# Carrying fourteen output columns over to the next steps, three heads per unit in the last steps, and kept tokens in five blocks of a two-layer recurrent attention kernel

## The chip, the core and the metric

The kernel runs on one core of one Trainium2 chip. A core has TensorE (PE, matrix products, with its weight loads listed apart as PEld), VectorE (DVE), ScalarE (ACT), GpSimd (POOL) and SyncE (SP); the last two also issue most of the transfers here. The metric is the device time of one execution in microseconds, as the median over several executions.

## The reference

There are two layers of the same kind, with the same weights. Each layer is a recurrent attention over segments of 32 tokens with 8 memory rows, followed by a gated feed-forward block (FFN). 2048 tokens of width 512 make 64 segments; there are 32 heads of width 128; the FFN is 1792 wide.

```python
for s in range(n_seg):                      # 64 segments, one after another
    h = concat([mem, x[32*s:32*s+32]])      # 8 + 32 = 40 rows
    q, k, v = h @ Wq, h @ Wk, h @ Wv        # 32 heads
    p = softmax(mask(q k^T * scale))        # memory rows seen by all, the rest causal
    o = (p v) @ Wo
    mem = o[:8]                             # the next segment's memory
    outs.append(o[8:])
# block B: (sigmoid(g) * u) @ w_down with g = h @ w_gate, u = h @ w_up
x = x + A(layernorm(x)); x = x + B(layernorm(x))     # layer 1
x = x + A(layernorm(x)); x = x + B(layernorm(x))     # layer 2
```

Only the 8 memory rows bind segment s+1 to segment s. Everything else of a segment depends on its own tokens.

## The kernel before, in words

**Steps.** `trace` emits 70 steps (`emit_step(t)`, t = 0 to 69). Step t computes segment t of the first layer (job j = 0) and segment t - 6 of the second (j = 1), as far as they exist: steps 0 to 5 have layer 1 alone, steps 6 to 63 both layers side by side in one moving operand of 80 columns, steps 64 to 69 layer 2 alone with 40 columns. Columns 0 to 39 belong to layer 1, 40 to 79 to layer 2; the last `NE` = 14 columns are the last 14 tokens of layer 2's segment. The last two two-layer steps are t = 62 and 63.

**Inside a step.** 32 heads go in groups of up to six. Line names are those of the profile of the kernel before:

- L874: Q and K of three heads, 8 weight-loaded matmuls a head; L910: scores. ACT casts Q and K to `qku`.
- L924 to L945: mask, maximum, subtraction, exponential, sum, reciprocal and product, on DVE with the exponential on ACT.
- L956: the probabilities of a *unit* (two or three heads side by side) are transposed on PE; L1226, L1228, L1234 and L1236 then spread the result over the diagonal blocks of `ptsb`, one copy for each of the two or three head rows.
- L982: probabilities times values, one matmul a unit and job; ACT casts the result to `otsb` (two buffers).
- L1001: the output product with `Wo`, 4 matmuls a head, 128 a step, all accumulated in one PSUM bank `WB`; its columns are the step's 40 or 80 columns. From `WB` DVE takes the next step's memory (L1014, L1019) and ACT takes the token columns to `oxT`, from which the FFN of a block of four segments starts.

Two-layer steps use units of three heads (`ni` = 3: 11 units, in groups of two); one-layer steps, at both ends, units of two (`ni` = 2: 16 units, in groups of three). The values lie in `vsb` in the layout of the unit. Most of V is computed ahead for whole blocks (L641, written to DRAM `scr` and read back); V of the rows that depend on the memory is made in the step as "strips" (L768, `sst`, then transfers into `vsb`).

**Saved columns at the start.** Steps 0 to 5 also compute Q and K of the first 14 tokens of layer 1's segment six steps later (54 columns in place of 40), keep them in `kx` and DRAM `xq`, and steps 6 to 11 load them and multiply 66 columns in place of 80. `kx` is not used after step 11.

**Blocks.** `pre1(b)` loads block b's tokens, applies the layer norm, transposes on PE (`layernorm_T`, L588 to L601) and writes `hT`. For some blocks the V rows of eight tokens fill spare columns of an earlier block's V pass: `v_fill(b, ...)` for b = 6, 9, 12, 14 and 15 loads the same tokens earlier and does the same layer norm and transposes once before. `ffn` runs the FFN (L1071 transposes, L1103 gate and up, L1126 down), whose weights are streamed by POOL from DRAM for each block into three rings `wg`, `wu`, `wd` of three tiles each. Before the first FFN the same nine tiles hold V on its way to `scr` ("boot"), and a key `"boot"` lets the first use of each ring wait until all those stores have left. `last_weights` loads the last block's weights into the rings and into the place of `Wv`.

**Order.** Every operation is a task handed to `Planner.add` with its engine (or two engines to choose from) and its keys. The order of all tasks is written out: `SEQUENCE` is a packed list of the order of all tasks and of the engine of each task that may run on two. `replay` walks that order, gives out tile slots and puts POOL's large transfers behind a PE instruction (`pace`); `warm` puts filler matmuls on a zero tile (`hot`, L1220) in front of a PE task where its own bookkeeping sees PE idle for over 250 ns in a thinly used stretch. Queues are in order on each engine; transfers go out on SP's or POOL's queue.

## Time and profile before

| | before |
|---|---|
| median of 3 runs | 1744.78 us (1743.07 to 1745.17) |
| the profiled execution's own time | 1748.87 us |
| its span, first to last instruction | 1746.8 us |
| PE busy, share of the span | 1733.3 us, 99% |
| DVE, ACT, POOL busy | 72%, 65%, 50% |
| instructions | 91,799 |
| matmuls | 39,151 |
| transfers | 273.41 MB, 157 GB/s on average |

Busy time is the union of the instructions' spans. [...] A row of the timeline merges instructions of one kind that follow one another: its start, the time from the first start to the last end, and the count.

### The profile page before, as it was taken

Reading aid. Unit: us, or ns where it says so; the run is one execution under the profiler, and the core shown is the slowest. Engines: PE = TensorE matmul, PEld = TensorE weight load, DVE = VectorE, ACT = ScalarE, POOL = GpSimd, SP = SyncE. Lnnn points to the kernel's source line nnn. Section 1 sums busy time; section 2 is a strip of 40 time slices with the busy share of each in tenths; the row PEclk is TensorE's granted clock in tenths of the full one; section 3 lists DMA queues with packets and bytes.
Section 4 is the critical chain, followed back from the end, with each engine's and each line's share of the span. In section 5 each row is a group of like instructions: output and inputs, shape, how many; then the busy total and the mean of one; then the engine's idle time right before and its main releaser. Section 6 shows DMA issues by size and latency. Waiting matters only on the chain.

```text
span 1746.8 us, 91799 instructions
## 1 busy us (share of the span) xinstructions
PE 1733.3 (99%) x39151; PEld 1492.4 (85%) x39151; DVE 1253.9 (72%) x4185; ACT 1143.3 (65%) x3142; POOL 873.5 (50%) x1402
## 2 busy tenths in 40 slices
PE   9999999999999999999999999999999999999998
PEld 4688789889888988989888888988888898888887
DVE  5677687677776776776677778776777776677776
ACT  3576777566666766676666667666766666666564
POOL 6535255535544564545455454545445454554453
PEclk9999999999999999999999999999999999999999
DMA  9835365655545464646456464646556454555544
GB/s 312 304 103 167 87 177 139 176 144 158 151 132 170 131 185 126 174 125 173 139 152 179 126 177 127 171 124 167 168 134 176 138 152 131 159 150 138 162 135 119
DMA packets 145071, 273.41 MB, mean 157 GB/s; under 512 B 39846, under 2 KB 85930, under 8 KB 144662
## 3 DMA queue, kind: packets, MB, share of 16 engines
q0 software_dynamic: 74144, 201.09, 40.5%
q1 hardware_dynamic: 70518, 66.46, 13.0%
q8 instruction: 307, 5.03, 1.2%
q14 instruction: 102, 0.84, 0.2%
HBM read 221.78 MB, written 27.07 MB: 142 GB/s over the span
## 4 chain that ended last, share of the span: by engine, by line
PE 94%; DMA 2%; issue 1%; SPq 1%; POOL 1%; ACT 0%; DVE 0%; POOLq 0%
PE bank L874 33%; PE bank L1001 17%; PE bank L1103 11%; PE bank L768 7%; PE bank L641 7%; PE bank L1126 5%; PE bank L910 4%; PE bank L982 4%; PE bank L956 2%; DMA wk_sb<-in_A_Wk_dram 1%; PE bank L601 1%; SPq L1230 1%; PE bank L1071 0%; DMA vsb<-sst 0%; DMA xs<-in_A_x_dram 0%
## 5 line engine op out<-in xcount | busy, mean ns | idle before, releaser
L874 PE MATMUL bank<-hT,wk_sb 128*128 128x80 bf16 (+3 forms) x8960 | 616.9, 198 | 2.3 <-DMA wk_sb<-in_A_Wk_dram 1.8
L874 PE MATMUL bank<-hT,wq_sb 128*128 128x80 bf16 (+3 forms) x8960 | 616.5, 198 | 0.6 <-DVE hT L1014 0.3
L1234 ACT CAST qku<-bank 128x480 bf16<-128x480 f32 (+3 forms) x770 | 383.6, 506 | 208.3 <-PE bank L874 183.7
L874 PEld LDWEIGHTS <-wq_sb 128*128 128x128 bf16 x8960 | 454.0, 99 | 31.6 <-issue 14.3
L874 PEld LDWEIGHTS <-wk_sb 128*128 128x128 bf16 x8960 | 447.5, 99 | 2.9 <-DMA wk_sb<-in_A_Wk_dram 1.9
L1001 PE MATMUL bank<-otsb,wo_sb 128*128 128x80 bf16 (+1 forms) x8960 | 356.2, 198 | 1.9 <-issue 1.9
L924 DVE TENSOR_TENSOR st<-bank,cst 40x240 f32<-40x240 f32 (+3 forms) x768 | 281.2, 368 | 101.2 <-PE bank L910 85.1
L1001 PEld LDWEIGHTS <-wo_sb 128*128 128x128 bf16 x8960 | 333.5, 99 | 12.4 <-issue 2.7
L1230 POOL DMA_DIRECT2D vsb<-sst x360 | 182.2, 510 | 185.9 <-ACT sst L1234 73.7
L1234 ACT CAST otsb<-bank 128x480 bf16<-128x480 f32 (+3 forms) x420 | 199.9, 482 | 83.0 <-PE bank L982 48.6
L1120 POOL DMA_DIRECT2D wd<-in_B_w_down_dram x217 | 156.9, 723 | 136.5 <-PE bank L1126 43.0
L1095 POOL DMA_DIRECT2D wg<-in_B_w_gate_dram x217 | 166.2, 766 | 113.3 <-PE bank L1103 54.7
L1096 POOL DMA_DIRECT2D wu<-in_B_w_up_dram x217 | 166.3, 767 | 108.1 <-PE bank L1103 34.5
L934 ACT ACTIVATE st<-st 80x240 f32<-80x240 f32 (+3 forms) x420 | 159.1, 381 | 70.2 <-DVE st L931 66.9
L1226 ACT ACTIVATE ptsb<-bank,small 80x160 bf16<-80x160 bf16 (+3 forms) x444 | 163.3, 385 | 16.4 <-PE bank L956 10.1
L1103 PE MATMUL bank<-xnT,wg 128*128 128x128 bf16 (+2 forms) x1784 | 171.4, 218 | 0.0
L1103 PE MATMUL bank<-xnT,wu 128*128 128x128 bf16 (+2 forms) x1784 | 171.0, 218 | 0.0
L936 DVE TENSOR_REDUCE small<-st 80x6 f32<-80x240 f32 (+3 forms) x420 | 151.6, 363 | 25.7 <-ACT st L934 23.6
L1230 POOL DMA_DIRECT2D vsb<-scr x197 | 104.7, 532 | 121.4 <-PE bank L982 62.0
L931 DVE TENSOR_TENSOR st<-st,small 80x240 f32<-80x240 f32 (+3 forms) x420 | 155.7, 372 | 7.7
L945 DVE TENSOR_TENSOR pb<-st,small 80x240 bf16<-80x240 f32 (+3 forms) x420 | 154.6, 371 | 7.3
L910 PE MATMUL bank<-qku 128*128 128x80 bf16 (+1 forms) x2240 | 158.6, 197 | 0.4 <-issue 0.4
(108 smaller groups left out, 2604.1 us busy)
## 6 DMA issues: line engine op xcount, KB each, us to landing
wg<-in_B_w_gate_dram POOLq DMA_DIRECT2D x220, 256.0 KB, 4.1
wu<-in_B_w_up_dram POOLq DMA_DIRECT2D x220, 256.0 KB, 4.2
wd<-in_B_w_down_dram POOLq DMA_DIRECT2D x220, 256.0 KB, 4.0
scr<-vst SPq DMA_DIRECT2D x90, 96.0 KB
vsb<-scr SPq DMA_DIRECT2D x120, 66.0 KB
vsb<-scr POOLq DMA_DIRECT2D x110, 66.0 KB, 3.5
vsb<-sst SPq DMA_DIRECT2D x190, 32.0 KB
vsb<-sst POOLq DMA_DIRECT2D x158, 32.0 KB, 2.7
```

The lines of the kernel that those rows point to most:

```text
L874: nc.tensor.matmul(o_ap, lhsT=W[:, c, h * P:(h + 1) * P], rhs=mv(c), start=(c == 0), stop=(c == DC - 1))
L910: nc.tensor.matmul(s_all(SB)[:, w0 + i, :], lhsT=fview(qku[:, i, 0, 0:1], [(1, P)]), rhs=qku[:, i, 1, 0:ncol], start=True, stop=True)
L924: pl.add("DVE", dve_ns(n, True), lambda gsz=gsz, hs=hs, st=st, SB=SB, pj_=pj_, npj_=npj_, mk=mk, idx=idx: nc.vector.tensor_tensor(out=st[p ...
L934: pl.add("ACT", act_ns(n), lambda hs=hs, st=st: nc.scalar.activation(out=st[pr, hs], in_=st[pr, hs], func=ACTF.Exp, scale=self.scale), r=s ...
L1001: nc.tensor.matmul(WB[:, c * ncol:(c + 1) * ncol], lhsT=self.wo[:, h, c * P:(c + 1) * P], rhs=otsb[:, hl, 0:ncol], start=(h == 0 and c == ...
L1095: pl.add("POOL", 760, lambda wg=wg, fs=fs: nc.gpsimd.dma_start(out=wg[:], in_=self.wgv[:, :, fs]), r=[("wo", self.H - 1)], w=[gk] + bt, la ...
L1096: pl.add("POOL", 760, lambda wu=wu, fs=fs: nc.gpsimd.dma_start(out=wu[:], in_=self.wuv[:, :, fs]), r=[("wo", self.H - 1)], w=[uk] + bt, la ...
L1103: nc.tensor.matmul(gu[:, 2 * i + k, 0:n], lhsT=W[:, c, i * P:(i + 1) * P], rhs=xnT[:, c, rw], start=(c == 0), stop=(c == DC - 1))
L1120: pl.add("POOL", 760, lambda wd=wd, ip=ip: nc.gpsimd.dma_start(out=wd[:], in_=self.wdv[:, 2 * ip:2 * ip + 2, :]), w=[dk] + (["boot"] if se ...
L1226: nc.scalar.activation(out=dst, in_=src, func=ACTF.Copy, scale=by)
L1230: {"SP": nc.sync, "POOL": nc.gpsimd}[tk.on].dma_start(out=got[1], in_=got[2])
L1234: nc.scalar.copy(out=dst, in_=src)
```

## The change

- In steps 62 and 63 (`put`) the output product leaves out the last 14 columns; 66 of 80 are multiplied. A copy per group puts those columns of `otsb` into half of `kx`. In steps 64 and 65 (`get`) a copy per group puts them beside the 40 columns of `otsb`, and the output product runs with 54 columns. The 14 columns' results go to `oxT` two steps later, by a small copy of their own.
- Steps 64 to 69 use units of three heads (`ni` = 2 only for t < 6): 11 units in place of 16, the value layout no longer changes at step 64, and `vsb` is filled in that layout.
- `v_fill`'s five blocks store their normalised, transposed tokens to DRAM (`xt`) through a `vst` tile; `pre1` of those blocks loads them into an `xn` tile (`kept_x`) and writes `hT` from there, with no second layer norm and no second transposes. It still loads the tokens themselves, for the residual.
- The three rings of three tiles become one pool of nine (`wtp`), and the `"boot"` key goes. The limits that `bank` had for two kinds of PSUM users (`"bg": 3, "v": 3`) go too.
- `SEQUENCE` is another one throughout.

By count of instructions: 39,153 matmuls become 39,090 (20 fewer layer-norm transposes, 30 fewer probability transposes, 30 fewer probability-times-value products, 17 more fillers); DVE 4,187 become 4,183, ACT 3,144 become 3,189, POOL 1,407 become 1,394, SP 1,065 become 1,077.

```diff
-        self.NG, self.ND = 3, 3
-        self.wg = [c.tile([P, DC, 2 * P], BF16, name=f"wg{i}") for i in range(self.NG)]
...
+        self.ND = 2
+        self.wt = [c.tile([P, 1024], BF16, name=f"wt{i}") for i in range(9)]
-        self.bank = Pool([...], {"bg": 3, "v": 3}, psum=True)
+        self.bank = Pool([...], psum=True)
+        self.wtp = Pool(self.wt)
...
     def ln_x(self, b, boot=True):
         if boot:
-            xb, key = self.boot_x[b]
+            return self.layernorm_T(self.boot_x[b][0][:, :], self.boot_x[b][1])
...
+        pst, B = self.layernorm_T(xb[:, :], key)
+        tt = pl.buf(self.vstp)
+        pl.add(("ACT", "DVE"), copy_ns(D, True), lambda: (tt[:, 0:D].rearrange("p (c n) -> p c n", c=self.DC), pst()), r=[B], w=[tt])
+        pl.add(("SP", "POOL"), {"SP": 430, "POOL": 590}, lambda: ("dma", self.xt[b * P:(b + 1) * P, :], tt[:, 0:D]), r=[tt], w=[("xt", b)], lat=3000.0, nb=P * D * 2)
+        self.kept.add(b)
+
+    def kept_x(self, b):
+        tt = pl.buf(self.xnp)
+        pl.add("SP", 430, lambda: nc.sync.dma_start(out=tt[:, :], in_=self.xt[b * P:(b + 1) * P, :]), r=[("xt", b)], w=[tt], lat=3500.0, nb=P * D * 2)
+        return (lambda: tt[:, :].rearrange("p (c n) -> p c n", c=self.DC)), tt
...
-        pst, B = self.layernorm_T(xb[:], ("xs", i))
+        pst, B = self.kept_x(b) if b in self.kept else self.layernorm_T(xb[:], ("xs", i))
...
-        ni = 3 if both else 2
+        ni = 2 if t < LAG else 3
...
+        put, get = self.NSEG - self.ND <= t < self.NSEG, self.NSEG <= t < self.NSEG + self.ND
+        wcol, half = ncol - NE if put else ncol + NE if get else ncol, 16 * (t % 2)
+        wrow = max(wcol, ncol)
...
+            if put:
+                pl.add(("ACT", "DVE"), copy_ns(gsz * NE, True), lambda ko=ko, hs=hs, otsb=otsb: (ko, otsb[:, hs, wcol:ncol]), r=[("otsb", oi)], w=kk)
+            if get:
+                pl.add(("ACT", "DVE"), copy_ns(gsz * NE, True), lambda ko=ko, hs=hs, otsb=otsb: (otsb[:, hs, ncol:wcol], ko), r=kk, w=[("otse", oi)])
...
-                            nc.tensor.matmul(WB[:, c * ncol:(c + 1) * ncol], lhsT=self.wo[:, h, c * P:(c + 1) * P],
-                                             rhs=otsb[:, hl, 0:ncol], ...)
+                            nc.tensor.matmul(WB[:, c * wrow:c * wrow + wcol], lhsT=self.wo[:, h, c * P:(c + 1) * P],
+                                             rhs=otsb[:, hl, 0:wcol], ...)
...
+        if get:
+            s = t - self.ND - LAG
+            dst = self.oxT[1][oi][:, :, (s % BLK + 1) * SEG - NE:(s % BLK + 1) * SEG]
+            pl.add("ACT", 110, lambda: (dst, wo3(ncol, NE)), r=[WB], w=[("oxT", 1, oi, s % BLK, "e")])
...
+    def weight(self, wt, nm, jp, keys, after):
+        self.pl.add("POOL", 760, lambda: nc.gpsimd.dma_start(out=wt[:, 0:1024].rearrange("p (c f) -> p c f", c=n), in_=src), w=keys, lat=4700.0, nb=370000, r=after)
```

## The prediction

> **What bounds the kernel now.** I read the page's totals and its chain of work, then windows by stage, then PE's own waits, and at last PE's timeline, for the price of each kind of matmul.

> ```profile
> PE   9999999999999999999999999999999999999998
> PE 94%; DMA 2%; issue 1%; SPq 1%; POOL 1%; ACT 0%; DVE 0%; POOLq 0%
> ```

> PE is busy in every slice, and the chain that ended last is 94% PE. A matmul less is time less, unless something else ends its stage. The stages (span, then PE's busy time; the last two columns are the transfers' share and GB/s):

> ```profile
> 0.00:50.00 50.00, 47.55 (x396) 22.92 (x397) 28.48 (x84) 19.36 (x41) 34.39 (x83) 1.00 0.97 322
> 50.00:100.00 50.00, 47.84 (x1080) 35.32 (x1079) 32.69 (x104) 29.22 (x100) 23.28 (x42) 0.97 0.72 238
> 150.00:200.00 50.00, 49.13 (x1175) 38.85 (x1170) 33.90 (x118) 34.59 (x109) 18.88 (x32) 1.00 0.48 134
> 200.00:250.00 50.00, 49.56 (x1185) 43.44 (x1182) 38.20 (x133) 36.12 (x112) 24.14 (x40) 1.00 0.48 134
> 1000.00:1050.00 50.00, 49.98 (x1124) 44.94 (x1121) 37.14 (x121) 31.68 (x88) 27.36 (x42) 1.00 0.58 161
> 1619.75:1746.80 127.05, 120.81 (x3456) 103.11 (x3454) 88.61 (x306) 72.32 (x241) 56.60 (x84) 1.00 0.49 139
> ```

> The start is bound by transfers (0.97 of the 16 engines). Its holes for PE are 2.45 and 2.16 us. Around the first FFN, 150 to 250 us, PE has 0.87 + 0.44 = 1.3 us of holes. The middle is full. The tail, from the first 40-column Q to the end, has 6.2 us of holes. The longest waits of PE itself:

> ```profile
> PE bank L1001 <- issue: 1.9, 2, 1.5
> PE bank L874 <- DMA wk_sb<-in_A_Wk_dram: 1.8, 1, 1.8
> PE bank L1126 <- DMA wd<-in_B_w_down_dram: 0.6, 1, 0.6
> ```

> **The change part by part.** Prices are distances from one row's start to the next row's, divided by the count.

> ```profile
> 1592.12 1.89 PE L1001 MATMUL bank<-otsb,wo_sb 128*128 128x80 bf16 x48
> 1593.84 0.20 PE L956 MATMUL bank<-cst,pb 80*128 80x80 bf16 x1
> ...
> 215.68 0.28 PE L874 MATMUL bank<-hT,wq_sb 128*128 128x66 bf16 x4
> ...
> 216.28 0.28 PE L874 MATMUL bank<-hT,wk_sb 128*128 128x66 bf16 x4
> ...
> 83.92 0.27 PE L874 MATMUL bank<-hT,wq_sb 128*128 128x54 bf16 x4
> ...
> 84.53 0.23 PE L910 MATMUL bank<-qku 128*128 128x40 bf16 x3
> ...
> 142.71 0.46 PE L1001 MATMUL bank<-otsb,wo_sb 128*128 128x40 bf16 x12
> 143.02 0.27 PE L982 MATMUL bank<-ptsb,vsb 80*128 80x80 bf16 x3
> ```

> *The 14 columns.* 80 columns cost 1.72 us / 48 = 35.8 ns. 66 columns cost 30.0 ns (five fours from 215.68 to 216.28 are 0.60 us for 20). 54 columns cost 0.61 us / 24 = 25.4 ns and 40 columns 0.31 / 12 = 25.8 ns, which is the same. So steps 62 and 63 save 2 x 128 x 5.8 ns = 1.5 us, and steps 64 and 65 do the columns for nothing, because a 40-column matmul already costs as much as a 54-column one.

> [...]

> ```profile
> 140.76 0.26 PE L956 MATMUL bank<-cst,pb 66*128 66x66 bf16 x3
> 140.86 0.39 PE L1103 MATMUL bank<-xnT,wg 128*128 128x128 bf16 x4
> ...
> 141.90 0.27 PE L982 MATMUL bank<-ptsb,vsb 80*128 80x80 bf16 x3
> 142.01 0.39 PE L1103 MATMUL bank<-xnT,wg 128*128 128x128 bf16 x4
> ...
> 1591.70 0.58 PE L982 MATMUL bank<-ptsb,vsb 120*128 120x120 bf16 x8
> ...
> 1624.63 0.38 PE L601 MATMUL bank<-cst,xn 128*128 128x128 bf16 x4
> 1624.85 0.26 PE L874 MATMUL bank<-hT,wq_sb 128*128 128x40 bf16 x4
> ```

> *Three heads per unit, six steps.* Transposes: 96 become 66, 30 x 31 ns (0.10 / 3, rounded down for the rows' two digits) = 0.9 us less. Products with V: 96 of 80 columns at 36 ns (3.5 us) become 60 of 120 columns at 52 ns (0.42 / 8, up to the output product at 1592.12) and 6 of 80 (together 3.4 us): 0.1 us less.

> *Kept tokens.* Five layer norms fewer take 20 transposes at 55 ns (0.22 / 4) off PE: 1.1 us.

> PE's work thus falls by 1.5 + 0.9 + 0.1 + 1.1 = 3.6 us. What the same parts put beside it:

> ```profile
> L1234 ACT CAST kx<-bank 128x84 bf16<-128x84 f32 (+1 forms) x48 | 10.2, 232 | 0.8 <-PE bank L874 0.6
> L1226 ACT ACTIVATE ptsb<-bank,small 80x160 bf16<-80x160 bf16 (+3 forms) x444 | 163.3, 385 | 16.4 <-PE bank L956 10.1 <-DVE ptsb L1228 3.0 <-DVE small L938 0.6
> L1234 ACT COPY ptsb<-bank 40x160 bf16<-40x160 bf16 (+1 forms) x268 | 71.7, 270 | 9.9 <-PE bank L956 6.6 <-PE bank L910 1.3 <-DVE ptsb L1228 0.4
> L588 DVE BATCH_NORM_STATS2 small<-xs 128x6 f32<-128x512 bf16 x36 | 24.6, 683 | 4.8 <-DMA xs<-in_A_x_dram 4.4
> ```

> 24 copies between `otsb` and `kx`, 12 in steps 62 and 63 and 12 in 64 and 65, about 0.23 us each (the `kx` row, same 84 columns): 2.8 us on ACT or DVE in some 75 us. Those into `kx` are read by nobody soon; ACT's next Q and K cast stands behind them, and ACT was busy 57% of the tail (72.3 of 127). Those into `otsb` stand before the output product, which then waits for two writers in place of one; but `kx` is ready two steps earlier and the copy can run beside the cast, so I take 0, with 12 x 0.23 = 2.8 us as the upper end and nothing below 0. The two extra `oxT` copies feed an FFN that starts after step 65 as before: 0.

> The one operation that lies on a path in the tail is the third spread. Five groups of six in each of six steps need three copies where they needed two: 30 more, 270 to 385 ns long. The units are two a group, so each copy is a third smaller. On two engines the third copy starts when one of the first two ends. Before it wait the product with V, `otsb`'s cast and the output product of that group. The cover is the Q, K and FFN matmuls that stand between; where they have run out, 0.3 us a group opens. Lower end 0; upper end 30 x 0.385 = 11.6 us. PE is busy 95% of the tail (120.81 of 127.05), so I take the spreads to lie open in the other 5%: 0.6 us.

> The values' strips reach `vsb` by six transfers a step in place of four, and the first group now needs three of them in place of two; the blocks' rows come by three in place of six.

> ```profile
> L1230 POOL DMA_DIRECT2D vsb<-sst x360 | 182.2, 510 | 185.9 <-ACT sst L1234 73.7 <-ACT st L934 24.2 <-DVE sst L1236 20.0
> ```

> One issue more ahead of the first group is 0.51 us on a queue in each of six steps: 0 while the softmax of that group takes longer, 3.1 us at most. PE's list of waits has no row of the tail for `vsb`, so I take 0.

> The kept tokens add five stores and five loads of 128 KB on SP's queue, one 512-column copy each, and the `hT` copies now wait for a transfer in place of the transposes; behind them on ACT and DVE the step's casts queue. They take 0.68 us and more of DVE for each layer norm away, and five rows of POOL.

> ```profile
> 78.87 0.36 SPq L730 DMA_DIRECT2D xvf<-in_A_x_dram  x1
> ...
> wd<-in_B_w_down_dram POOLq DMA_DIRECT2D x220, 256.0 KB, 4.0
> ```

> Ten issues at 0.36 us are 3.6 us of SP over most of the run; a landing takes about 4 us, and `pre1` stands a whole block, four steps, ahead of the first use. I take 0. Uncovered, one late landing is 4 us, five are 20.

> *Pool, key and order.* Nine common tiles without the key let the first weights leave as soon as one tile is free: in the changed kernel's order the first of them stands 17 places earlier on POOL's queue. What waits there now, in the chain of waits:

> ```profile
> 152.63 2.52 issue
> ...
> 157.03 2.97 issue
> 160.03 3.48 DMA wd<-in_B_w_down_dram
> ```

> The holes of this stage are 1.3 us; at best all go, at worst the stores that the weights now overtake come late by as much. I take half of them as gain: 0.7 us. The rest of the order is permuted everywhere; in the full middle that can gain nothing (0.02 us of holes in 50). The start is bound by the same weights before and after, so 0 there, between its two holes' 4.6 us gained and as much lost.

> The 17 added fillers (ten of 512 columns, three of 384, two of 256, two of 128) are put where the kernel's list has PE idle. A 512-column matmul costs 0.86 / 4 = 0.215 us here:

> ```profile
> 1590.12 1.02 PE L1126 MATMUL bank<-wd,hff 128*128 128x512 bf16 x4
> 1590.98 0.38 PE L982 MATMUL bank<-ptsb,vsb 120*128 120x120 bf16 x4
> ```

> They are 5,120 + 1,152 + 512 + 256 columns, 3.0 us of PE. In the changed order some 1.8 us of fillers stand in the first step, which has none before, and 2.8 us in the six last steps, against 0.5 before. I take them as lying in waits that exist in both kernels: 0, upper end 3.0 us.

> Sum: -3.6 + 0.6 - 0.7 = -3.7 us. The profiled execution took 1748.87 us (span 1746.8 and 2.1 around it), so 1745.2 for such an execution; that one lies 4.1 us over the median, and against the median of 1744.78 the sum gives **1741.1 us**.

> **The rivals.** *The order gains more (24%).* Holes at the start (4.6 us), at the first FFN (1.3) and the pause in the last output product,

> ```profile
> 1730.68 0.34 PE L1001 MATMUL bank<-otsb,wo_sb 128*128 128x40 bf16 x7 [1.46 <-issue]
> ```

> are 7.4 us; half of them gone, with nothing lost in the tail, gives 3.6 + 3.7: 1737.5. For it: the whole list is new, and freer pools stand behind it. Against it: the start waits for transfers.

> *The fillers lie in new holes (14%).* Then 3.0 us come back: -3.7 + 3.0 gives 1744.1, no change that can be measured. For it: the place of the fillers, in the last FFN above all, where none stood before.

> *The tail is bound by the third spread (15%).* If the cover is gone, the 30 spreads open 0.385 us each, 11.6 us, and 3.6 + 0.7 come off: 1752.1. It turns the sign once more than 4.3 of 11.6 us, about 37% of the spreads, lie open; half of them give 1746.3. For it: layer 2 alone has one recurrence and little to run between. Against it: PE's 95% in the tail.

> [...]

> **How the numbers follow.** My sum has 44%. A measurement of this kernel can tell about 0.2%, 3.5 us: below 1741.3 is faster, above 1748.3 slower. The sum lies just beyond that line, so of its 44% I give 31 to faster and 13 to no change; the first rival adds 24 to faster; the fillers 9 to no change and 5 to slower; the spread 15 to slower; the weight load 3 to no change. Faster 55%, same 25%, slower 20%. The sum's own range is 1738.5 to 1743.5. The range of 8 in 10 reaches down over the first rival with a little of the start, 1736, and up past the fillers to half of the spreads, 1746.5.

> **What would show it.** In the changed profile: 256 output-product rows of 66 columns 30 ns apart, and 256 of 54 columns at 25; 66 transposes in the last six steps; no second layer norm for the five blocks and no PE wait that ends with `xn<-xt`; fewer holes between 150 and 250 us; the tail, from the first 40-column Q to the end, about 0.5 us shorter than 127.05. Wrong would be: a tail of over 129 us, waits of L982's line for `ptsb`, or fillers followed by waits at the same places.

## The result, and the profile after

The changed kernel takes 1752.57 us (median of 6, 1750.09 to 1754.21) against 1743.92 us of the kernel before on the same chip (median of 6, 1741.78 to 1746.97). The ratio is 1.0047, with a 95% interval of 1.0034 to 1.0061: slower by 8 us, where 1741.1 was forecast. In a second comparison (x9 below) it was 1.0033 (1.0022 to 1.0044). So the change costs about 6 to 8 us by the two ratios, and PE's work was to fall by 3.6. The profiled execution took 1753.03 us, with a span of 1751.3.

The chain of work, PE's slices and the instruction queue on the page of the changed kernel:

```profile
PE   9999999999999999999999999999999999999999
PE 92%; DMA 3%; DVE 2%; issue 1%; ACT 1%; POOL 1%; SPq 0%; DVEq 0%; POOLq 0%; ACTq 0%
q8 instruction: 307, 5.03, 1.2%
```

The chain was 94% PE before and is 92% now: more of the end hangs on waits. The stages (stretch, span, busy time of PE, PEld, DVE, ACT and POOL with instructions, PE's granted clock, transfers' share, GB/s), the last from the first 40-column Q to the end:

```profile
0.00:50.00 50.00, 46.41 (x382) 22.15 (x383) 29.30 (x79) 18.45 (x44) 30.42 (x76) 1.00 0.95 314
50.00:100.00 50.00, 47.02 (x1067) 34.37 (x1063) 30.47 (x102) 30.34 (x100) 26.69 (x48) 1.00 0.80 258
150.00:200.00 50.00, 49.04 (x1194) 39.18 (x1190) 33.80 (x118) 34.81 (x110) 15.87 (x27) 1.00 0.49 135
200.00:250.00 50.00, 47.82 (x1134) 41.72 (x1131) 36.39 (x133) 34.10 (x104) 22.62 (x36) 1.00 0.49 139
1000.00:1050.00 50.00, 50.00 (x1132) 44.74 (x1125) 35.10 (x117) 33.74 (x90) 26.65 (x41) 1.00 0.56 163
1623.19:1751.25 128.06, 122.66 (x3408) 103.03 (x3406) 89.39 (x314) 78.42 (x277) 52.44 (x77) 1.00 0.46 134
```

PE's holes grew: by 1.1 us in the first 50 us and 0.8 in the next 50, where no change was forecast, and to 3.1 us in place of 1.3 between 150 and 250, where they were to shrink. The tail is 128.06 us long, not 0.5 shorter than 127.05 but 1.0 longer, and PE is busy in it for 1.85 us more although the edits leave it less to do there. PE's waits, longest sums first:

```profile
PE bank L891 <- issue: 2.5, 4, 0.9
PE bank L999 <- DMA scr<-wt: 1.5, 1, 1.5
PE bank L891 <- DMA wq_sb<-in_A_Wq_dram: 1.5, 1, 1.5
PE bank L1133 <- ACT otsb L1262: 1.2, 1, 1.2
...
PE bank L999 <- DMA wt<-in_B_w_gate_dram: 1.0, 1, 1.0
```

The edited operations do what the prediction priced. Groups of the last stretch, shapes apart, and the timeline around one row of each output product:

```profile
L1024 PE MATMUL bank<-otsb,wo_sb 128*128 128x66 bf16 x256 | 9.5, 193 | 0.0
L1024 PE MATMUL bank<-otsb,wo_sb 128*128 128x54 bf16 x256 | 8.0, 186 | 0.0
L973 PE MATMUL bank<-cst,pb 66*128 66x66 bf16 x66 | 7.9, 194 | 0.1
```

```profile
1600.29 1.14 PE L1024 MATMUL bank<-otsb,wo_sb 128*128 128x66 bf16 x32
1601.27 0.61 PE L1133 MATMUL bank<-xnT,wt 128*128 128x128 bf16 x8
...
1638.43 1.07 PE L1024 MATMUL bank<-otsb,wo_sb 128*128 128x54 bf16 x36
1639.34 0.22 PE L973 MATMUL bank<-cst,pb 66*128 66x66 bf16 x2
```

66 columns start 0.98 / 32 = 30.6 ns apart, 54 columns 0.91 / 36 = 25.3 ns, while one matmul's span is 193 and 186 ns on average (the groups' rows above); so the price is read from the starts. There are 66 transposes. By the counts of all operations and these distances PE's work, fillers aside, falls by 3.6 us, as forecast. The question of the study is where that went, and 6 to 8 us besides.

### The profile page after: what moved, and what is told of

Same layout as the page of the kernel before. It is cut to its first block, busy times and chain, and to the rows that moved or that the text cites. A ratio compares the mean times of both kernels' runs of the same rounds, so it can differ in the third digit from the quotient of the medians.

```text
span 1751.3 us, 91725 instructions
## 1 busy us (share of the span) xinstructions
PE 1731.9 (99%) x39088; PEld 1488.6 (85%) x39088; DVE 1257.3 (72%) x4181; ACT 1148.9 (66%) x3187; POOL 865.1 (49%) x1389
## 4 chain that ended last, share of the span: by engine, by line
PE 92%; DMA 3%; DVE 2%; issue 1%; ACT 1%; POOL 1%; SPq 0%; DVEq 0%; POOLq 0%; ACTq 0%
PE bank L891 33%; PE bank L1024 17%; PE bank L1133 11%; PE bank L640 7%; PE bank L779 7%; PE bank L1154 5%; PE bank L927 4%; PE bank L999 4%; PE bank L973 2%; PE bank L600 1%; DVE st L941 1%; DMA kx<-xq 0%; DMA wq_sb<-in_A_Wq_dram 0%; PE bank L1104 0%; DMA wo_sb<-in_A_Wo_dram 0%
## 5 line engine op out<-in xcount | busy, mean ns | idle before, releaser
L1024 PE MATMUL bank<-otsb,wo_sb 128*128 128x80 bf16 (+3 forms) x8960 | 354.2, 198 | 0.1
L1133 PE MATMUL bank<-xnT,wt 128*128 128x128 bf16 (+2 forms) x3568 | 243.1, 219 | 1.2 <-ACT otsb L1262 1.2
L1063 POOL DMA_DIRECT2D wt<-in_B_w_up_dram x220 | 168.0, 764 | 108.1 <-PE bank L973 25.1
L1063 POOL DMA_DIRECT2D wt<-in_B_w_gate_dram x220 | 168.1, 765 | 105.2 <-PE bank L927 23.6
L1063 POOL DMA_DIRECT2D wt<-in_B_w_down_dram x220 | 158.7, 721 | 115.7 <-PE bank L973 26.3
L1133 PEld LDWEIGHTS <-wt 128*128 128x128 bf16 x3568 | 205.6, 98 | 7.7 <-issue 2.5
L1254 ACT ACTIVATE ptsb<-bank,small 80x160 bf16<-80x160 bf16 (+4 forms) x466 | 166.8, 379 | 21.7 <-PE bank L973 14.2
L953 DVE TENSOR_REDUCE small<-st 80x6 f32<-80x240 f32 (+3 forms) x420 | 151.9, 362 | 23.2 <-ACT st L951 20.3
L946 DVE TENSOR_REDUCE small<-st 80x6 f32<-80x240 f32 (+3 forms) x420 | 152.9, 365 | 7.9
## 6 DMA issues: line engine op xcount, KB each, us to landing
wt<-in_B_w_up_dram POOLq DMA_DIRECT2D x220, 256.0 KB, 4.1
wt<-in_B_w_gate_dram POOLq DMA_DIRECT2D x220, 256.0 KB, 4.0
wt<-in_B_w_down_dram POOLq DMA_DIRECT2D x220, 256.0 KB, 4.0
```

The lines of the kernel that those rows point to most:

```text
L946: pl.add("DVE", dve_ns(n), lambda hs=hs, st=st, mx=mx: nc.vector.tensor_reduce(out=mx[pr, hs], in_=st[pr, hs], axis=AX.X, op=ALU.max), r=s ...
L1024: nc.tensor.matmul(WB[:, c * wrow:c * wrow + wcol], lhsT=self.wo[:, h, c * P:(c + 1) * P], rhs=otsb[:, hl, 0:wcol], start=(h == 0 and c == ...
L1063: self.pl.add("POOL", 760, lambda: nc.gpsimd.dma_start(out=wt[:, 0:1024].rearrange("p (c f) -> p c f", c=n), in_=src), w=keys, lat=4700.0, ...
L1133: nc.tensor.matmul(gu[:, 2 * i + k, 0:n], lhsT=W[:, (2 * c + i) * P:(2 * c + i + 1) * P], rhs=xnT[:, c, rw], start=(c == 0), stop=(c == DC ...
L1254: nc.scalar.activation(out=dst, in_=src, func=ACTF.Copy, scale=by)
```

## Experiments

All kernels but x9, which is the changed kernel once more, come from one source; a run's name starts with its number (x1, x2, ...). Four switches turn the edits on one by one: `CARRY` (14 columns), `THREE` (three heads), `KEEP` (kept tokens) and `NINE` (pool of nine tiles, no start key). The order of the tasks can be taken from the kernel before ("old"), from the changed one ("new"), or spliced at a step. Ratios are to the kernel before on the same chip, with 95% intervals; 0.1% is 1.75 us.

### One source, everything off, and the pool alone

```diff
-CARRY, THREE, KEEP, NINE = 1, 1, 1, 1   # new order
+CARRY, THREE, KEEP, NINE = 0, 0, 0, 0   # x1: old order
+CARRY, THREE, KEEP, NINE = 0, 0, 0, 1   # x5, and again x10: old order
```

> The kernel before once more, written with switches that are all off, so that every engine gets the same instructions in the same order. It measures what the comparison itself is worth, and gives a second profiled execution of the old order: the first was 1748.87 us, over every timed run but one near it. Expected: 1744 us, a ratio of 1.000 within 0.001. If the profiled execution is near 1744 us, the places in which it gains on the first one are noise and no part of the difference; if it is again near 1749 us, a profiled execution of the old order is some 5 us slower than a plain one.

> The kernel before with one edit: its nine weight tiles are one pool, without the key that made the first weight loads wait for all stores of the start, and without the caps on banks. The order on every engine is the old one. If the edit of the pool itself costs the 3 us of the start: ratio 1.0017. If it is the new order that costs them: 1.000, or a little less where a load may now start sooner (0.999 to 1.000).

> The old order with the pool of nine tiles alone, a second time. The first time gave 1.0015 (1.0003 to 1.0026) though its profile shows no wait that is longer than before. If the pool costs time by itself: 1.001 to 1.002 again. If the first time was chance: 1.000 within 0.001.

Measured: x1 1.0000 (0.9989 to 1.0012), so the source adds nothing of its own. The pool alone gave 1.0015 (1.0003 to 1.0026) and, on another chip, 1.0014 (1.0005 to 1.0024). The pool, which was to gain 0.7 us together with the key and the order, costs about 2.5 us. Every other operation and its place in the order is as before, but for three fillers fewer.

Three things are in that switch: the missing start key, the missing limits on PSUM users, and that a weight takes the tile that has been free longest, of any of the three old rings. The key and the waits of the rings were each put back alone, on the old order; the limits stay off in both:

```diff
+BOOT = 1     # x14: the first weights wait for the V stores again
...
+                    if BOOT and self.nxt("bootg", 999) < 3:
+                        ks[0].append("boot")
+                        ks[1].append("boot")
```

> The pool alone on the old order, but the first nine weight loads wait again for all stores of the start; the waits of the rings stay away. If the missing key is what costs (weights that come early fill the DMA engines at 140 to 190 us, and TensorE pauses between two multiplications of a group at 115, 121, 149, 171 and 190 us, as in the traces with the pool): 1.000. If the freer choice of tiles costs: 1.0014.

```diff
+RING = 1     # x11: a weight also waits for the reader of the third weight of its kind before it
...
+                    gr = [("ring", q, self.nxt("ring" + q, 3)) for q in ("wg", "wu")] if RING else []
+                    ks = [wg] + gr[:1], [wu] + gr[1:]
...
+                pl.add("PE", 2 * DC * mm_ns(n), mm, r=[xk, gk, uk] + (gr if RING and not last else []), w=[GB])
```

> The pool alone, on the old order, but each weight load also waits, as before, for the multiplications with the weights three loads earlier in its own ring; the key of the start stays away. Theory: the pool costs time because its weight loads leave earlier (the tile used longest ago is free sooner than the next one of a ring) and hold up the smaller transfers. Then 1.000 here, against 1.0015 with the pool free. If the missing key of the start is what costs, or the choice of tiles: 1.0015 here too.

Measured: with the key 1.0013 (1.0004 to 1.0022), as slow as without; with the rings' waits 0.9995 (0.9986 to 1.0005), on the same chip as x10. So the loss lies in weights that leave as soon as any tile is free, earlier than the three rings let them. The traces show the earlier start: ACT has the same instructions in the same order in x10 and x11, and set against these, 128 of the 672 weight loads leave over 1 us earlier in x10, and none over 1 us later. The choice of tiles, the missing key and the missing limits cost nothing that can be seen, as x11 has all three. What the earlier loads hold up is not settled. In the profiles, the pool alone shows holes around the first FFN that x1 does not have. PE's waits from 126 to 195 us, first x1, then x10:

```profile
PE bank L1173 <- DMA wt<-in_B_w_down_dram: 0.5, 1, 0.5
```

```profile
PE bank L897 <- issue: 2.1, 1, 2.1
PE bank L1005 <- DMA vsb<-sst: 1.8, 1, 1.8
PE bank L785 <- issue: 1.3, 1, 1.3
```

But these holes do not go with the time. From 100 to 250 us PE is idle for 1.4 us in the kernel before, 2.2 in x1 and 7.2 in x10; but also for 4.0 in x11, which has the old time, and for only 1.7 and 3.2 in x12 and x4 (below), which have the pool and the old order in that stretch. One profile of each does not carry a difference of 2.5 us here.

### Which stretch of the order

```diff
-SEQUENCE = new order, all edits
+SEQUENCE = new to the first scores of step 9, then old      # x2: pool only
+SEQUENCE = old to the first scores of step 9, then new      # x3: all edits
+SEQUENCE = old to step 62, then new                         # x4: 14 columns, three heads, pool
+SEQUENCE = old, new from step 9 to step 62, old             # x12: kept tokens, pool
```

> The order of the changed kernel up to the first QK of step 9 (its start and its first feed-forward block, with the pool of nine weight tiles), the old order from there on; no carried columns, no third head per unit, no kept tokens, so TensorE's work is that of the kernel before. Theory 1 (the new order makes TensorE wait where the two profiles part, +2.7 us by step 9): 1746.7 us, and up to 1752 us if the whole loss is in the start. Theory 2 (the edits of the end cost the time, by the third spread in the chain of each group): 1744 us, no change. Theory 3 (the new order waits in the middle, at transfers): 1744 us, no change.

> The other half: the old order up to the first QK of step 9, the order of the changed kernel from there on, with all of the edits (3.58 us less work for TensorE, as in the changed kernel). Theory 1 in its strong form (all is lost in the start): 1744 - 3.6 = 1740.4 us; as the two profiles part it keeps 4.2 - 2.7 = 1.5 us of the loss: 1745.5 us. Theories 2 and 3 (end or middle): 1752.5 us, as the changed kernel.

> The old order up to the first QK of step 62, the order of the changed kernel from there on, with the carried columns and three heads per unit, but without kept tokens: 2.5 us less work for TensorE. Theory 2 (the end's edits): 1752.5 us or more. Theory 1 or 3: the end alone, which is 0.8 to 1.2 us longer in the profile of the changed kernel than in that before: 1745 us.

> The old order up to the first QK of step 9 and from step 62 on, the order of the changed kernel between them, with the pool and the kept tokens and without the edits of the end: 1.12 us less work for TensorE. By the two profiles that the earlier runs left, the new middle loses 2.6 to 5.1 us to late V rows (steps 12, 26, 38, 52) and late weights (step 57): +1.5 to +4 us, 1.001 to 1.0023, and with the pool's 0.0015 on top if that is not the same loss: up to 1.0035. If the middle is not at fault: 0.9994 (the saved 1.1 us), or 1.001 with the pool's loss.

Measured: x2 1.0017 (1.0008 to 1.0027), x3 1.0028 (1.0017 to 1.0039), x4 1.0011 (1.0003 to 1.0020), x12 1.0027 (1.0017 to 1.0037). Each holds the pool's 0.0014. What is left is 0.4 us for the start, 2.2 us for the middle, which should have gained the kept tokens' 1.1 us, and -0.6 us for the end, which should have gained 1.9 (1.5 + 0.9 + 0.1 - 0.6). Each of these differences is uncertain by about 2 us, so only the middle's is clear of zero, and that barely. The parts add up to 1.4 + 0.2 + 1.3 - 0.3 = 2.6 thousandths, 4.5 us; the whole measured 3.3 to 4.7. The rest is within the intervals of four differences and is not placed.

### The middle: values that come late

PE's waits of x12 around the first product with V of step 38, then of step 52, and of x7 (all of the new order, described below) at step 38:

```profile
PE bank L1006 <- DMA wt<-in_B_w_up_dram: 2.6, 1, 2.6
```

```profile
PE bank L1006 <- DMA wt<-in_B_w_gate_dram: 1.1, 1, 1.1
```

```profile
PE bank L1005 <- DMA vsb<-sst: 1.8, 1, 1.8
```

L1006, like L1005 there, is the product of probabilities and values; it reads no weight. In x12 the profile names the transfer that it saw land last; what the matmul needs is `vsb`, as x7's row says outright. SP's queue ahead of that matmul (at 987.1 us) in x12:

```profile
977.88 3.10 SPq L1279 DMA_DIRECT2D vsb<-sst  x5
981.07 0.54 SPq L1279 DMA_DIRECT2D xt<-vst  x1
981.66 1.75 SPq L1279 DMA_DIRECT2D vsb<-sst  x2
983.53 0.48 SPq L1279 DMA_DIRECT2D vsb<-scr  x1
984.05 0.51 SPq L1279 DMA_DIRECT2D vsb<-sst  x1
```

The store of block 14's kept tokens (`xt<-vst`, 131 KB) and a load of V rows for the next step stand ahead of some of the last three strips. The first of these three lands just before the product starts: in x12 it was issued at 981.66 and landed 5.4 us later, at 987.03. In x3, x7 and x9 the same strip took 4.9 to 5.2 us to land, and its issue alone held SP for 1.1 to 1.8 us in all four. In x1, with the old order, the strip at that place took 2.0 us and landed 2.9 us ahead of the product. At step 52 an FFN output store (131 KB), a token load and a V load stand ahead of the last strip.

PE was idle before the first product with V of step 38 for 2.6 us in x12, 1.9 in x3, and 1.8 in x7 and x9. The changed kernel's own first profile has the same order on SP and no such wait: there the strip took 3.8 us. It shows the wait at step 52 (the w_gate row of 1.0 us above). So the wait is in four of these five profiles, not in all. That the strip is late because of the store and POOL's 256 KB weight loads beside it is an inference from the order; the test is to move the store.

In x3, x7 and x9 the hole was followed by something more. Windows of x9 around step 38, columns as before:

```profile
984.00:986.00 2.00, 2.00 (x47) 1.99 (x44) 1.86 (x6) 1.62 (x7) 0.84 (x2) 1.00 0.98 332
986.00:988.00 2.00, 0.23 (x4) 0.10 (x1) 1.26 (x5) 0.20 (x1) 0.75 (x1) 1.00 0.72 194
988.00:990.00 2.00, 1.89 (x35) 1.77 (x35) 0.75 (x3) 1.39 (x4) 0.64 (x1) 0.89 0.32 115
990.00:992.00 2.00, 2.00 (x23) 1.44 (x21) 1.65 (x7) 0.78 (x3) 0.86 (x2) 0.50 0.49 133
992.00:994.00 2.00, 2.00 (x41) 2.00 (x39) 0.44 (x2) 1.12 (x5) 0.71 (x1) 0.76 0.55 158
994.00:996.00 2.00, 2.00 (x59) 2.00 (x56) 1.36 (x5) 1.61 (x5) 1.19 (x2) 1.00 0.30 111
```

PE is idle for 1.8 us from 986, and from 989.6 its granted clock is half for 3.4 us: 23 matmuls in 2 us in place of 47 to 60. At half the clock these 3.4 us do the work of 1.7, so by this estimate the hole costs its length and up to another 1.7 us.

The test leaves all edits where they are and moves only five transfers on SP's queue behind the strips of their step:

```diff
-step 38 on SP: ..., xt<-vst, vsb<-sst, vsb<-sst, vsb<-scr, vsb<-sst
+step 38 on SP: ..., vsb<-sst x8, xt<-vst, vsb<-scr
-step 52 on SP: out store, vsb<-scr and xs<-x load ahead of the last vsb<-sst
+step 52 on SP: the three behind the last vsb<-sst
```

> The middle of the changed kernel between the old start and the old end, as measured at 1.0027, with the five transfers of steps 38 and 52 moved behind the V rows of their step. Theory (late V rows are the middle's loss): the waits of 2.8 and 1.2 us go, 1.0005 to 1.0015. If the order of the middle costs elsewhere: 1.0027.

> The changed kernel with five of SyncE's transfers moved back by some places: in step 38 the store of block 14's kept tokens and one V row load of step 39, in step 52 a store of 131 KB, a load of tokens and one V row load of step 53. They now leave behind the last V rows of their step instead of ahead of them. Nothing else moves. In four traces the first multiplication with V of step 38 waited 1.9 to 2.8 us (in three of them followed by 3.4 us at half the granted clock, worth 1.7 us), that of step 52 1.2 us. If these waits are the middle's loss: 2.5 to 4 us less than the changed kernel, 1.0010 to 1.0025 of before. If the middle's order costs elsewhere: 1.0033 to 1.0047 as it is.

x18 (x12 so mended) ran 1.0008 (0.9999 to 1.0018) against x12's 1.0027: 3.3 us less, with an uncertainty of about 2.4. The same place on SP's queue in x18:

```profile
980.39 6.37 SPq L1285 DMA_DIRECT2D vsb<-sst  x8
986.87 0.54 SPq L1285 DMA_DIRECT2D xt<-vst  x1
987.51 0.40 SPq L1285 DMA_DIRECT2D vsb<-scr  x1
```

PE has no wait between 984 and 994 us nor between 1335 and 1345 there; the strip landed 3.9 us after its issue and 0.5 us ahead of the product. So in the middle by itself the late strips account for the loss. With them mended it lies 0.6 thousandths under the pool alone, which fits the kept tokens' 1.1 us but is within the error. In the whole changed kernel the gain is not shown: there the same five moves (x13) gave 1.0028 (1.0017 to 1.0039) against 1.0033 for its repetition, 0.9 us less with an uncertainty of 2.7, where 2.5 to 4 us were expected. PE's only row near step 38 is `vsb<-scr`, 0.2 us, so the waits went and the time hardly moved.

### The changed kernel again, and its end

```diff
 # x9: the changed kernel itself
-CARRY, THREE, KEEP, NINE = 1, 1, 1, 1
+CARRY, THREE, KEEP, NINE = 0, 0, 1, 1   # x7: new order, 14 columns and three heads undone
```

> The changed kernel once more, beside the runs it is compared with: 1.0047 within 0.0015. If it comes out near 1.0030, the run with the end's edits undone (1.0030) is no longer faster than it, and nothing speaks against these edits.

> The order of the changed kernel all through, with kept tokens and the pool, but with the carried columns and the third head per unit undone: 2.47 us more work for TensorE than in the changed kernel, no third spread. If the loss is in the order and the two edits of the end are worth what they take off: 1.0047 + 0.0014 = 1.006. If the two edits cost the 1.9 us that the new end lost: 1.0036 or less.

x9 measured 1.0033 (1.0022 to 1.0044), x7 1.0030 (1.0017 to 1.0042). In the new order the end's two edits, 2.5 us of PE work, are worth nothing that can be seen, though the error of this difference is nearly 3 us.

```diff
-CARRY, THREE, KEEP, NINE = 0, 0, 0, 1   # old order
+CARRY, THREE, KEEP, NINE = 1, 0, 0, 1   # x6: the 14 columns alone
```

> The old order with the pool and the carried columns alone: steps 62 and 63 give 54 instead of 80 columns... in their second half's output rows, steps 64 and 65 take 54 for 40, no third head per unit, no kept tokens. TensorE has 1.47 us less to do by the durations of before (35.8 ns for 80 columns, 30.0 for 66, 25.4 for 54 and 40). If the edits are worth what they take off and the loss lies in the order: 1.5 us under the run with the pool alone, 0.9991 of before. If the copies to and from the kept tile hold up the output multiplications (72 copies, some 0.2 us each): 1.000 to 1.004.

x6 measured 1.0006 (0.9995 to 1.0018), 0.8 to 0.9 thousandths under the pool alone: the 1.5 us of the prediction, though the error is larger, and x15 below does not repeat it. (The two steps multiply 66 columns, and the trace has 24 copies, not the 54 and 72 of the expectation.)

```diff
-return (dst, pt[:, :, 0:nj, :]) + ((self.lower[i][r], "scaled") if i else ())
+return (dst, pt[:, :, 0:nj, :]) + ((self.lower[i][r], "twice" if i == 2 and t >= self.NSEG else "scaled") if i else ())
```

> The changed kernel with the third spread of each of the 36 groups of the last six steps issued twice, one after the other: some 10.6 us more work on ScalarE and VectorE (25 at 0.327 us, 11 at about 0.22 us), nothing else. If the end is bound by the chain through the spreads: up to 10.6 us longer, 1.0108 of before. If TensorE's other work covers them: 1.0047 to 1.006.

Here every third spread of the last six steps is done twice. By the trace that is 30 spreads and 9.5 us more on ACT and DVE, a little less than expected. It measured 1.0043 (1.0030 to 1.0057) against 1.0047 and 1.0033 without. PE's waits for `ptsb` after 1575 us in x8, of which the changed kernel has none after 1600:

```profile
PE bank L1006 <- ACT ptsb L1274: 1.2, 4, 0.4
PE bank L1006 <- DVE ptsb L1284: 0.3, 1, 0.3
PE bank L1006 <- ACT ptsb L1282: 0.2, 1, 0.2
```

So even doubled, at most a fifth of it shows as PE's waiting, 1.7 of 9.5 us; done once, the third spread lies beside other work.

Then the fillers. Those on the zero tile after 1597 us, before and then after (count, shortest, median and longest ns, first and last start, shapes):

```profile
L1220 PE MATMUL bank<-hot x3: 270/323/376, 1659.1 to 1709.6; 128*128 128x512 bf16 x1, 128*128 128x256 bf16 x1, 128*128 128x384 bf16 x1
```

```profile
L1248 PE MATMUL bank<-hot x17: 219/378/391, 1622.7 to 1738.6; 128*128 128x512 bf16 x10, 128*128 128x384 bf16 x4, 128*128 128x256 bf16 x2, 128*128 128x128 bf16 x1
```

By their columns these are 0.5 us before and 3.1 us after. From the first Q of step 62 to the end of the last matmul the old order takes 171.5 to 174.1 us in seven profiles, the new one 172.8 to 174.6 in four (the changed kernel, x9, x4 and x3). Up to 3.9 us of each are issue rows, pauses that differ from one profile of the same kernel to the next: after 1575 us they are 0.9 us in the changed kernel's first profile and 0.5 in x9 (the last section takes them up). Less these, the two groups part: 169.7 to 170.2 us in all seven with the old order, 171.8 to 172.7 in the four with the new one. So the end has 2.5 us less work by the edits, 2.6 us more fillers, and takes about 2 us more. Do the fillers take time, or fill it?

```diff
+            fill = {k: v for k, v in fill.items() if self.pl.tasks[k].start < 1600000.0}
```

> The changed kernel without its 17 filler multiplications after 1600 us (3.08 us of TensorE by their columns; the kernel before has three there, 0.5 us). If the fillers lie in holes in which TensorE waits for the chain of a group: the time stays (1.0033 to 1.0047), TensorE's idle time in the end rises by 3.1 us, or the clock is halved after a hole and it is slower. If the fillers hold up work: up to 3.1 us less, 1.0016 to 1.003.

x17, with no fillers in the end, measured 1.0042 (1.0028 to 1.0056): no gain is seen, though its error is nearly as large as the 3.1 us of fillers. In its trace the end, less the issue rows, takes 170.9 us, so some 1.2 of the 3.1 us come back, and PE's other waits of over 0.15 us rise from 1.1 us (the changed kernel and x9) to 1.8; they are for `hT`, `hff`, `ptsb` and `xn`. So the larger part of the fillers lies in waits. Even without them the end is 0.9 us longer than the old one, whose waits of this kind are 0.3 to 0.5 us, with 2.5 us less work: the saved work became room in it. That it is the chain of operations of a group (probabilities, product, casts, memory) that sets this time is argued from these rows; no run takes the chain apart.

### Everything mended

```diff
-CARRY, THREE, KEEP, NINE = 0, 0, 0, 1 ; RING = 1   # x11
+CARRY, THREE, KEEP, NINE = 1, 0, 0, 1 ; RING = 1   # x15: old order, rings' waits, 14 columns
```

> The old order with the carried columns and the pool with the waits of the rings: the 1.47 us that the carried columns take off TensorE, without the pool's loss. 0.9995 - 0.0008 = 0.9987 of before; if the carried columns save nothing: 0.9995 to 1.000. A candidate to beat both kernels.

```diff
-SEQUENCE = old to the first scores of step 9, then new               # x3
+SEQUENCE = the same, five transfers later ; BOOT = 1                 # x16
```

> All of the edits: the old order up to the first QK of step 9 with the key of the start, then the order of the changed kernel with the five transfers of steps 38 and 52 moved back. It was 1.0028 without the key and the moves. If both mends hold (0.0014 and 0.0015 to 0.0023): 0.999 to 1.000. If neither matters: 1.0028.

x15 measured 0.9996 (0.9987 to 1.0004), no less than x11's 0.9995: the 14 columns' 1.5 us do not show there, where 0.9987 was expected. x16 measured 1.0021 (1.0012 to 1.0030), 0.7 thousandths under x3 and far from the 0.999 to 1.000 expected. That expectation counted on the start key to mend the pool, which x14 shows it does not; all edits with the rings' waits and the five moves was not run. No version measurably beats the kernel before.

## Why the prediction was wrong, point by point

What failed is what was set against PE's saved work: the term "pool, key and order" was -0.7 us and its pool alone measured +2.5, the full middle's order was 0 and measured +2.2, and the end's work was counted as time, -1.9, where x4's time shows -0.6 and the traces about +2. By the times these and the start's 0.4 add up to 4.5 us of the 6 to 8; the rest is open.

**Right: PE's prices.** The 14 columns (30.6 and 25.3 ns against 30.0 and 25.4), the 66 transposes, the five layer norms (31 in place of 36 of the `xs` statistics) and so the 3.6 us of PE work. No run shows a weight load that sets the distance, to which the forecast gives 3%: 80 columns stood 35.8 ns apart before, 66 columns 30.6 and 54 columns 25.3 after.

**Right: what was costed at nothing, or little, by its cover.** The third spread (0.6 us; x8), the copies between `otsb` and `kx`, the strips of the last steps (no wait for them in the tail), and the kept tokens' loads, which landed 29.65 us or more ahead of their first use. PE's matmuls with V have one wait for `ptsb`, 0.3 us, and it lies before 600 us.

**Wrong: "pool, key and order", -0.7 us.** The pool is +2.5 (x5, x10, x14, and x11 as the counter-test). I argued from the first weights alone, as holes to be filled or stores to be late by the same 1.3 us, and never asked what the other weight loads, which also leave sooner (128 of 672 by over 1 us), collide with. The holes between 150 and 250 us, of which half were to go, rose from 1.3 to 3.1 us; what the pool's loads hold up stays open.

**Wrong: "the rest of the order is permuted everywhere; in the full middle that can gain nothing", 0.** It cannot gain, but it can lose, and I had set no bound on that side. The middle lost 2.2 us net, 3.3 gross by x12 and x18. One of the stores that I costed by "ten issues at 0.36 us" is among the five transfers that did it: I asked whether its own data come in time, and not what stands behind it on SP. Its 0.54 us of issue and 131 KB stand ahead of strips that the next matmul waits for, beside weight loads. x18 moved all five at once, so the share of the store alone is not measured.

**Wrong: the saved work of the end as saved time, -2.5 + 0.6 us.** The end gained 0.6 us by x4's time, within its error of 2, and by the traces it takes 2 us more. The rival "the fillers lie in new holes" (14%) named the mechanism and was near in size (2.6 us more fillers, about 2 us longer); x17 shows that most of that time stays as waits when the fillers go. The row that warned was the 6.2 us of holes in the tail: in a stage in which PE already waits, PE work taken out need not shorten it.

**The start, 0 with 4.6 us to either side.** The new order there costs 0.4 us by x2, within its error, so 0 stands. The changed kernel's profile has 46.41 us of PE in the first 50 us against 47.55.

The rival that turned the sign in the forecast, the third spread, was the wrong one. As far as the runs show it, the sign was turned by transfers that leave at other times: the pool's weight loads and the late strips.

## What to carry to other kernels

A load that leaves earlier is not free: here 128 of 672 weight loads of 256 KB left over 1 us sooner, and the looser pool cost about 2.5 us where 0.7 was to be gained, so ask of every transfer that a change releases or moves what stands behind it and lands beside it. PE work saved in a stage with holes need not come out as time: here 2.5 us less work left an end about 2 us longer, in a tail that had 6.2 us of holes; look at what ends PE's waits there before counting it. When a written-out order is replaced as a whole, give its middle a loss of a few late landings, even where the old one shows none: here they were PE waits of 1.8 to 2.6 us at step 38 and of 1.0 to 1.1 at step 52.

## What the runs showed of the hardware

**Pauses in the middle of a group.** Most of PE's "issue" rows are pauses in which the profile shows nothing that is waited for. Count PE's instructions in order, two a matmul and the separate waits: in the profile before and the changed kernel's first one, 11 of the 12 issue rows over 0.15 us lie where that count stands at 194 or 195 over a multiple of 256. Each of these runs passes 307 such places, and on both pages the instruction queue has 307 packets. Only 6 and 5 of the places pause so long, for up to 1.46 us each and 3.0 and 3.1 us in sum; x10 has a pause of 2.1 us. Which of them do differs between profiles of one kernel: the changed kernel's first profile has one of 0.46 us at 115.9 us, and x9 is idle for 0.19 us in all from 100 to 120. The 1.46 us in the last output product before, which the first rival of the prediction hoped to gain, is one of them. Windows of x10 around the two largest:

```profile
145.00:147.00 2.00, 1.85 (x59) 1.52 (x55) 0.52 (x2) 0.50 (x2) 1.24 (x2) 1.00 1.06 278
147.00:149.00 2.00, 0.03 (x2) 0.02 (x1) 0.00 (x0) 0.39 (x2) 0.27 (x1) 1.00 0.99 265
149.00:151.00 2.00, 2.00 (x48) 2.00 (x47) 0.00 (x0) 0.62 (x3) 0.60 (x1) 0.52 0.39 122
...
169.86:171.12 1.26, 0.00 (x1) 0.00 (x1) 0.00 (x0) 0.43 (x1) 1.16 (x2) 1.00 0.00 0
```

PE stands still for 2.1 us while the transfers' share is 0.99 to 1.06, and half the clock follows; but it also stands still for 1.26 us from 169.86 with no transfer at all, so full transfer engines are not what makes these pauses. At some 300 of the 307 places no such pause shows; the others are large enough to hide a change of this size in one profile, as in the ends compared above. Nor are they shown as the cause of the pool's loss: from 126 to 195 us x11 has 1.6 us of issue rows, against 3.4 in x10 and none before, and ran as fast as before (0.9995).
